# Sliding-window attention in rounds of three items instead of one or two, ahead of two expert layers

## The chip, the cores and the metric

The kernel runs on one NeuronCore of a Trainium2 chip. The metric is the device time of one execution in microseconds (us), as the median of several runs. Engines: PE is TensorE (matmuls and transposes; PEld its weight loads), DVE is VectorE, ACT is ScalarE, POOL is GpSimd, SP issues most DMAs. Each engine works through its own instructions in order; semaphores tie the engines together.

## The reference

Attention over q, k, v of shape (4 batches, 8 heads, 576 positions, 64 wide) in fp32, with a causal window of 128 positions and a linear distance bias per head; then a soft mixture of 8 experts with a balancing loop; then one dense layer pair.

```
scores = q @ k.T / sqrt(64)                       # per batch and head
mask   = (0 <= i - j) & (i - j < 128)
attn   = softmax(where(mask, scores - slope[h] * (i - j), -1e9))
x      = (attn @ v) laid out as (2304 tokens, 512)
P      = exp(x @ w_gate - max); 8 times: rows and columns of P scaled to fixed sums
x      = sum_e P[:, e] * (relu(x @ w1[e]) @ w2[e])      # w1[e] 512x1024, w2[e] 1024x512
h      = x @ w_in;  g = h, 0 or (h + 1)^2 / 4 by h's range
out    = g @ w_out
```

## The kernel before, in words

Matmuls that need precision are made of three (`mm3`, lines 74 to 76): high part by high part, high by low, low by high. The time falls into three stretches. Attention takes the first 223 us or so; the rest of a first expert unit and the balancing loop follow until about 272 us; the experts and the dense pair take what is left. The change touches attention alone.

**Items.** Attention is cut into 80 items: 16 head pairs `g` (4 per batch) times 5 blocks `i` of query rows (four of 128 rows, the last, `i == FULL`, of 64 rows, both heads of the pair stacked in one 128-row tile). Block 0 sees 128 keys, blocks 1 to 3 see 256, the last 192. An item goes through five steps:

- S, `a_scores`: matmuls into two PSUM banks, one per head (tags `s0`, `s1`); then DVE reads them with the bias added and the row minimum taken (L327).
- E, `a_exp`: ACT takes the exponential of each head (L336).
- N, `a_norm`: DVE makes the reciprocal of the row sums (L341, L342), POOL multiplies (L343).
- T, `a_turn`: PE transposes the item's weights into one bank of tag `t` (L355), which has two buffers; ACT copies out the first key block (L359), DVE the second (L361). An item of block 0 has only the first.
- O, `a_out`: PE multiplies by v (L375) into one bank of tag `o`; ACT copies the high part out (L383), DVE makes the low part (L386).

**Other work in a round.** P, `a_prep`: a pair's q and k are transposed (three parts: two with four transposes, one, the tail, with two) into a bank of tag `p` (one buffer), in the first batch also tag `g`; ACT makes the high part (L298), DVE the low (L301). Loads of later pairs (`a_load`) are issued on SP behind a pair's third part. B: one step of the weight preparation `u0_weights`. F: the filler, a few steps of a first expert unit (`unit0`: three matmuls a step, into the two banks of tag `g`); it may begin on a block of rows when enough items are through O (`step[0]`, first block after the 8th item), and gets 1.8 steps per item.

All eight PSUM banks are taken: `g` 2, `p` 1, `s0`, `s1`, `t` 2, `o` 1.

**Rounds.** The order of all engines' queues is written out by hand: in each round the letters of `START` or `ORDER` are emitted in sequence, and `BEHIND` says how many items an operation stands behind S. A round takes one item while the item's number is under 20, then two:

```
START, ORDER, NSTART = "EBSNFPOT", "ESONTPBFP", 20
BEHIND = [{"S": 0, "E": 1, "N": 1, "T": 3, "O": 4}, {"S": 0, "E": 2, "N": 2, "T": 4, "O": 6}]
two = new >= NSTART
new += 1 + two
```

That makes 20 rounds of one, 30 of two, and 3 more to empty the pipeline.

Of the kernel before, what the change touches and what calls it, by code (L numbers as in the profile page):

```python
# [19 lines left out]
P = 128  # L20
# [9 lines left out]
def attn_moe_ffn(ctx: ExitStack, tc, q, k, v, w_gate, w1, w2, w_in, w_out, out):  # L30
# [171 lines left out]
    TAIL = [slice(0, P // 2), slice(P // 2, P)]  # L202
    nat, QK, st, atT = {}, {}, {}, {}
    tails, QT = {}, {}

    def tail_at(g):
        return g if g < NPAIR else NPAIR + g % 2
# [9 lines left out]
    def a_load(g, ap):  # L217

        b, hp = divmod(g, NPAIR)
        for nm, src in (("q", q), ("k", k)):  # L220
            t = ap.tile([P, FULL, P], F32, tag=f"n{nm}", bufs=2, name=f"n{nm}")
            for j in range(2):
                sj = src[b, 2 * hp + j]
                nc.sync.dma_start(out=t[:, 0:FULL, j * D:(j + 1) * D],
                                  in_=sj[0:FULL * P, :].rearrange("(c p) d -> p c d", p=P))
            nat[g, nm] = t
        tail_load(g)

    def rows(src, b, i, h0, h1):
        x, n = QB[i]  # L230
# [26 lines left out]
        for g in range(NPAIR):  # L257
            tail_load(g)

    def a_prep(g, ap, part):  # L260

        b, hp = divmod(g, NPAIR)
        if part == 0:
            r = B - 1 - hp // 2
            for n, nm in enumerate("qk"):
                if r > b:
                    x, c0 = (xh, xl)[hp % 2], r * SQ
                    QK[g, nm] = [x[:, 2 * n + m, c0:c0 + SQ] for m in range(2)]
                else:
                    QK[g, nm] = [ap.tile([P, SQ], F32R, tag=f"{nm}{x}", bufs=3, name=f"{nm}{x}") for x in "hl"]  # L270

        if b == 0 and count[0] % 3:
            ps = ps_pools[0].tile([P, 512], F32, tag="g", bufs=2, name="pst")
        else:
            ps = ps_pools[0].tile([P, 512], F32, tag="p", bufs=1, name="pst")
        count[0] += 1
        if part == 2:
            todo = [("q", FULL, NQ, 0), ("k", FULL, NQ, P)]
            for n, nm in enumerate("qk"):
                nc.tensor.transpose(ps[:, n * P:(n + 1) * P], tails[nm, tail_at(g)], ident)  # L280
            QT[g] = [ap.tile([P, P], F32R, tag=f"qt{x}", bufs=4, name=f"qt{x}") for x in "hl"]
        elif b == 0:
            todo = [("q", 2 * part, 2 * part + 2, 0), ("k", 2 * part, 2 * part + 2, 256)]
        else:
            todo = ([("q", 0, 4, 0)], [("k", 0, 4, 0)])[part]
        for nm, i0, i1, c0 in todo if part < 2 else ():
            for i in range(i0, i1):
                x, n = QB[i]
                nc.tensor.transpose(ps[:, c0 + x - i0 * P:c0 + x - i0 * P + n], nat[g, nm][:n, i, :], ident[:n, :n])
        low = []  # L290
        for nm, i0, i1, c0 in todo:
            scale = SCALE if nm == "q" else 1.0
            s0, s1 = QB[i0][0], QB[i1 - 1][0] + QB[i1 - 1][1]
            h, l = (t[:, s0:s1] for t in QK[g, nm])
            pc = ps[:, c0:c0 + s1 - s0]
            if part == 2 and nm == "q":
                (h, l), pc = QT[g], ps[:, 0:P]
            nc.scalar.activation(h, pc, AF.Copy, scale=scale)  # L298
            low.append((l, pc, scale, h.bitcast(F32), ALU.mult, ALU.subtract))
        for x in low:  # L300
            nc.vector.scalar_tensor_tensor(*x)  # L301

    def a_scores(some, ap, bias):

        PS = [ps_pools[0].tile([P, 2, 2 * P], F32, tag=f"s{j}", bufs=1, name="pss") for j in range(2)]
        made = []
        for x, (g, i) in enumerate(some):
            q0, nq = QB[i]
            k0 = max(0, q0 - P)
            nk = q0 + nq - k0  # L310
            made.append((nq, nk, P if i == 0 else 0))
            (qh, ql), (kh, kl) = QK[g, "q"], QK[g, "k"]
            if i == FULL:
                mm3(PS[0][:, x, :nk], *QT.pop(g), kh[:, k0:k0 + nk], kl[:, k0:k0 + nk], True, True)
                continue
            for j in range(2):
                hs = slice(j * D, (j + 1) * D)
                mm3(PS[j][:nq, x, :nk], qh[hs, q0:q0 + nq], ql[hs, q0:q0 + nq], kh[hs, k0:k0 + nk], kl[hs, k0:k0 + nk],
                    True, True)
        for x, (g, i) in enumerate(some):  # L320
            nq, nk, c0 = made[x]
            h0 = 2 * (g % NPAIR)
            s = ap.tile([P, 2, 2 * P], F32, tag="s", bufs=6, name="s")
            mx = ap.tile([P, 8], F32, tag="mx", bufs=8, name="mx")
            nj = 1 if i == FULL else 2
            for j in range(nj):
                nc.vector.tensor_tensor_reduce(  # L327
                    out=s[:, j, :nk], in0=PS[j][:, x, :nk],
                    in1=bias[:, h0 + j, c0:c0 + nk] if nj == 2 else tbias[:, g % NPAIR, :], scale=-1.0,
                    scalar=3.0e38, op0=ALU.add, op1=ALU.min, accum_out=mx[:, j:j + 1])  # L330
            st[g, i] = (s, mx, nk, nj)
# [14 lines left out]
    def a_turn(g, i, ap):  # L346

        s, mx, nk, nj = st.pop((g, i))
        kbs = [i] if i == 0 else [i - 1, i]
        ps = ps_pools[0].tile([P, 2, 2, P], F32, tag="t", bufs=2, name="psat")  # L350
        at = ap.tile([P, 2, 2, P], F32, tag="at", bufs=4, name="at")
        for c, kb in enumerate(kbs):
            n = QB[kb][1]
            for j in range(nj):
                nc.tensor.transpose(ps[:n, c, j, :], s[:, j, c * P:c * P + n], ident)  # L355
        for c, kb in enumerate(kbs):
            n = QB[kb][1]
            if c == 0:
                nc.scalar.activation(at[:n, c, 0:nj, :], ps[:n, c, 0:nj, :], AF.Copy)  # L359
            else:  # L360
                nc.vector.tensor_copy(at[:n, c, 0:nj, :], ps[:n, c, 0:nj, :])  # L361
        atT[g, i] = (at, kbs)

    def a_out(some):
        PS = ps_pools[0].tile([P, 2, P], F32, tag="o", bufs=1, name="pso")
        low = []
        for x, (g, i) in enumerate(some):
            b, hp = divmod(g, NPAIR)
# [416 lines left out]

    START, ORDER, NSTART = "EBSNFPOT", "ESONTPBFP", 20
    BEHIND = [{"S": 0, "E": 1, "N": 1, "T": 3, "O": 4}, {"S": 0, "E": 2, "N": 2, "T": 4, "O": 6}]
    SHARE = 1.8  # L790
    PREP0 = [-1, 3, 4, 0, 5, 6, 1, 7, 8, 2, 9, 10]
    PREP = [11, 14, 17, 20, 29, 34, 37, 41, 53, 56, 59, 67]
    LAG = (5, 4, 4, 5, 6, 6, 6, 6)
    with tc.manual_schedule():
        nc.gpsimd.memset(small, 0.0)
# [2 lines left out]
        make_identity(nc, ident)  # L798

        NG = B * NPAIR  # L800
        items = []
        for b in range(B):
            for c in ((0, 1), (2, 3, 4)) if b < B - 1 else (range(NQ),):
                items += [(g, i) for g in range(b * NPAIR, (b + 1) * NPAIR) for i in c]
        NI = len(items)
        preps = sorted((y, *divmod(n, 3)) for n, y in enumerate(PREP0) if n)
        preps += [(PREP[g - NPAIR] + x, g, x) for g in range(NPAIR, NG) for x in range(3)]

        blocks = [(7, 0, 256), (19, 256, 256), (27, 512, 256), (39, 768, 384), (47, 1152, 256), (59, 1408, 256),
                  (79, 1664, 384), (79, 2048, 256)]  # L810
# [6 lines left out]
        with tc.tile_pool(name="ac", bufs=1, side="right") as ac, tc.tile_pool(name="ap", bufs=2, side="right") as ap, \  # L817
# [72 lines left out]
            while done["O"] < NI:  # L890
                s += 1
                step[0] = done["O"]
                two = new >= NSTART
                new += 1 + two
                order = ORDER if two else START
                for pos, op_ in enumerate(order):
                    some = ()
                    if op_ in done:
                        end = max(done[op_], min(new - BEHIND[two][op_], NI))
                        some = items[done[op_]:end]  # L900
                        done[op_] = end
                    if op_ == "S":
# [8 lines left out]
                        if s == 3:  # L911
                            for x in range(NPAIR, NPAIR + 2):
                                a_load(x, ap)
                        if s == 2:
                            fast.append(u0_weights(wp))
                        if s == 9:
# [8 lines left out]
                        for x in some:  # L925
                            a_turn(*x, ap)
                    elif op_ == "B":
                        advance(fast, 2 * (1 + two))
                    elif op_ == "F":
                        credit += SHARE * (1 + two) / order.count("F")  # L930
                        while credit >= 1.0:
                            credit -= 1.0
                            state = next(work)
                            if state == "wait":
                                credit = 0.0
                    elif op_ == "P":
                        if s == max(PREP0) + 1:
                            p0.close()
                            hp = p1b.enter_context(tc.tile_pool(name="hp", bufs=1))
                            op = p1b.enter_context(tc.tile_pool(name="op", bufs=2))  # L940
                        for _, pg, x in [y for y in preps if y[0] < new][:1]:
                            preps.pop(0)
                            a_prep(pg, ap, x)
                            if x == 2 and NPAIR <= pg < NG - 2:
                                a_load(pg + 2, ap)
                    elif op_ == "O" and some:
                        a_out(some)
                        for g, i in some:
# [109 lines left out]
```

## Time and profile before

| | us |
|---|---|
| median of 3 runs | 2064.2 (2062.78 to 2064.44) |
| profiled execution | 2063.22 |
| its span, first to last instruction | 2061.5 |
| PE busy in the span | 2039.0 (99%) |
| DVE, ACT, POOL busy | 1250.0, 703.7, 485.0 |

The profile comes from one execution. A busy PE counts a matmul from its start to its modelled end, and these overlap; how close PE is to its best is seen from the distance between the starts of neighbouring matmuls, not from its busy share.

### The profile page before, as it was taken

What the parts mean: (1) busy time and instruction counts of PE and PEld (TensorE: products, weight loads), DVE (VectorE), ACT (ScalarE), POOL (GpSimd) and SP (SyncE); (2) the same over time, 40 slices, a digit from 0 to 9 for tenths busy, and PEclk for the clock granted to TensorE, in tenths of its full rate; (3) what the DMA queues carried; (4) which work ended last, traced back from release to release, by engine and by line L of the source; (5) the groups of instructions that cost most, each with busy time, mean ns of one, the idle gap of its engine ahead of it and who ended that gap; (6) DMA issues with size and microseconds to landing.
All of it is one profiled execution on the core that took longest, in us unless ns stands there. A gap on an engine that the chain in (4) does not pass through costs nothing.

```text
span 2061.5 us, 30122 instructions
## 1 busy us (share of the span) xinstructions
PE 2039.0 (99%) x11071; PEld 1830.9 (89%) x11071; DVE 1250.0 (61%) x2916; ACT 703.7 (34%) x1657; POOL 485.0 (24%) x522
## 2 busy tenths in 40 slices
PE   7999999999999999999999999999999999999999
PEld 5888889989989889889999899899899898998998
DVE  6766656545545766666566665666665565656645
ACT  6767443333333332112112132122121134553543
POOL 5333347666666601111111100101110000000000
PEclk9999999999999999999999999999999999999999
DMA  7331448767776657667667566676675454555552
GB/s 158 85 86 48 141 160 296 264 247 252 257 257 246 255 209 280 232 233 251 232 229 247 216 220 247 230 257 224 225 263 190 181 192 184 198 208 184 219 189 108
DMA packets 180132, 432.83 MB, mean 210 GB/s; under 512 B 69648, under 2 KB 93712, under 8 KB 179984
## 3 DMA queue, kind: packets, MB, share of 16 engines
q1 hardware_dynamic: 168080, 411.37, 57.0%
q10 hardware_dynamic: 11904, 19.53, 2.9%
q8 instruction: 87, 1.43, 0.3%
q14 instruction: 61, 0.50, 0.1%
HBM read 311.44 MB, written 119.01 MB: 209 GB/s over the span
## 4 chain that ended last, share of the span: by engine, by line
PE 93%; DVE 3%; DMA 1%; SPq 1%; issue 1%; ACT 0%; POOL 0%; ACTq 0%; DVEq 0%; POOLq 0%
PE psg L74 16%; PE psg L76 16%; PE psg L75 16%; PE psc L74 4%; PE psd L74 4%; PE psc L75 4%; PE psc L76 4%; PE psd L75 4%; PE psd L76 4%; PE psb L74 3%; PE psa L75 3%; PE psb L75 3%; PE psb L76 3%; PE psa L76 3%; PE psa L74 3%; PE pso L375 2%
## 5 line engine op out<-in xcount | busy, mean ns | idle before, releaser
L74 PE MATMUL psg<-w2h,hh 128*128 128x512 f32 x1368 | 533.7, 390 | 0.1
L76 PE MATMUL psg<-w2h,hl 128*128 128x512 f32 x1368 | 532.8, 389 | 0.0
L75 PE MATMUL psg<-w2l,hh 128*128 128x512 f32 x1368 | 532.2, 389 | 0.0
L734 DVE SCALAR_TENSOR_TENSOR acc<-psg,pt,acc 128x512 f32<-128x512 f32 x252 | 187.9, 749 | 247.7 <-PE psg L76 245.9
L76 PEld LDWEIGHTS psg<-w2h,hl 128*128 128x128 f32 x1368 | 256.8, 188 | 53.4
L74 PEld LDWEIGHTS psg<-w2h,hh 128*128 128x128 f32 x1368 | 256.8, 188 | 51.8 <-DVE acc L734 1.3
L75 PEld LDWEIGHTS psg<-w2l,hh 128*128 128x128 f32 x1368 | 256.9, 188 | 50.8
L662 ACT ACTIVATE hh<-c 128x384 fp32r<-128x384 f32 x270 | 140.9, 522 | 90.9 <-DVE c L700 57.4
L664 DVE SCALAR_TENSOR_TENSOR hl<-c,hh 128x384 fp32r<-128x384 f32 x270 | 161.2, 630 | 0.0
L74 PE MATMUL psc<-xh,w1h 128*128 128x384 f32 x456 | 155.2, 340 | 1.6 <-DVE u L689 1.6
L76 PE MATMUL psc<-xh,w1l 128*128 128x384 f32 x456 | 154.9, 340 | 0.0
L74 PE MATMUL psd<-sh,w1h 128*128 128x384 f32 x456 | 153.6, 337 | 1.2 <-DVE c L692 0.8
L75 PE MATMUL psc<-xl,w1h 128*128 128x384 f32 x456 | 154.8, 339 | 0.0
L75 PE MATMUL psd<-sl,w1h 128*128 128x384 f32 x456 | 153.0, 336 | 0.0
L76 PE MATMUL psd<-sh,w1l 128*128 128x384 f32 x456 | 152.9, 335 | 0.0
L683 ACT ACTIVATE p<-psa 128x384 f32<-128x384 f32 x57 | 28.1, 494 | 355.7 <-PE psa L76 353.2
L80 POOL TENSOR_TENSOR dl<-e,dh 128x128 fp32r<-128x128 f32 (+1 forms) x64 | 43.2, 683 | 353.2 <-ACT dh L79 345.0
L80 POOL TENSOR_TENSOR w2l<-raw,w2h 128x512 fp32r<-128x512 f32 x60 | 81.4, 1379 | 119.6 <-ACT w2h L79 119.6
L686 DVE TENSOR_TENSOR u<-psb,p 128x384 f32<-128x384 f32 x57 | 31.7, 557 | 111.9 <-PE psb L76 91.5
L79 ACT ACTIVATE dh<-e 128x128 fp32r<-128x128 f32 (+1 forms) x64 | 23.7, 387 | 220.3 <-DVE e L162 216.2
L343 POOL TENSOR_TENSOR s<-s,mx 128x512 f32<-128x512 f32 (+2 forms) x80 | 66.7, 850 | 124.9 <-DVE mx L341 77.1
L74 PEld LDWEIGHTS psd<-sh,w1h 128*128 128x128 f32 x456 | 85.7, 188 | 2.4 <-DVE c L692 1.4
(220 smaller groups left out, 4071.9 us busy)
## 6 DMA issues: line engine op xcount, KB each, us to landing
w1h<-wd1h SPq DMA_DIRECT2D x84, 896.0 KB, 4.7
w1l<-wd1l SPq DMA_DIRECT2D x84, 896.0 KB, 6.8
w2h<-wd2h SPq DMA_DIRECT2D x84, 512.0 KB, 5.1
w2l<-wd2l SPq DMA_DIRECT2D x84, 512.0 KB, 5.9
raw<-in_moe_w SPq DMA_DIRECT2D x60, 512.0 KB, 4.4
wd1h<-w1h SPq DMA_DIRECT2D x30, 896.0 KB, 6.0
wd1l<-w1l SPq DMA_DIRECT2D x30, 896.0 KB, 6.5
wd2h<-w2h SPq DMA_DIRECT2D x30, 512.0 KB, 6.0
```

What stands on the lines that cost most here:

```text
L74: nc.tensor.matmul(ps, lhsT=lh, rhs=rh, start=first, stop=False, skip_group_check=on)
L75: nc.tensor.matmul(ps, lhsT=lh, rhs=rl, start=False, stop=False, skip_group_check=on)
L76: nc.tensor.matmul(ps, lhsT=ll, rhs=rh, start=False, stop=last, skip_group_check=on)
L79: nc.scalar.activation(h, x, AF.Copy)
L80: eng.tensor_tensor(l, x, h.bitcast(F32), ALU.subtract)
L343: nc.gpsimd.tensor_tensor(s[:, 0:nj, :nk], s[:, 0:nj, :nk], mx[:, 6:6 + nj].unsqueeze(2).to_broadcast([P, nj, nk]), ALU.mult)
L375: nc.tensor.matmul(PS[hs, x, :nq], lhsT=nat[b, "v", kb][:n, (2 * hp + j) * D:(2 * hp + j + 1) * D], rhs=at[:n, c, 0, TAIL[j]] if i == FULL ...
L662: nc.scalar.activation(h, c, AF.Relu)
L664: V.scalar_tensor_tensor(l, c, 0.0, h.bitcast(F32), ALU.max, ALU.subtract)
L683: nc.scalar.activation(p1, pa, AF.Copy)
L686: V.tensor_tensor(u2, pb, p1, ALU.add)
L734: nc.vector.scalar_tensor_tensor(a, ps, sc, a, ALU.mult, ALU.add)
```

## The change

From the ninth round on a round takes up to three items. The items of a batch are regrouped: blocks 0 and 1 of its pairs are mixed so that a round's score tiles fill a 512-column bank per head, and blocks 2, 3 and FULL of one pair make a round; the FULL scores go to the bank of tag `p`. The last batch mixes differently. Behind the same first 8 rounds of one there are 25 rounds (22 with three items, 3 with two), then 3 to empty the pipeline. `BEHIND` counts rounds now.

In a round the first E takes at most two items and the second, `e`, the third, with an N behind each. All P of a round stand in one place, behind T and these; a second and third P of a round use the banks of tag `t`. There is one P list per round number (`PREP`), and the loads of the pair after next are issued behind part 1 (the tails behind part 2). The third item of a round, where it is a narrow one, gets smaller tiles (`short`). The shares of the filler and its gates stay.

```diff
-        if b == 0 and count[0] % 3:
-            ps = ps_pools[0].tile([P, 512], F32, tag="g", bufs=2, name="pst")
-        else:
-            ps = ps_pools[0].tile([P, 512], F32, tag="p", bufs=1, name="pst")
+        if part < 2 and g < NPAIR and count[0] % 3:
+            tag = "g"
+        ps = ps_pools[0].tile([P, 512], F32, tag=tag, bufs=1 if tag == "p" else 2, name="pst")
...
-        PS = [ps_pools[0].tile([P, 2, 2 * P], F32, tag=f"s{j}", bufs=1, name="pss") for j in range(2)]
+        PS = [ps_pools[0].tile([P, 512], F32, tag=f"s{j}", bufs=1, name="pss") for j in range(2)]
...
             if i == FULL:
-                mm3(PS[0][:, x, :nk], *QT.pop(g), kh[:, k0:k0 + nk], kl[:, k0:k0 + nk], True, True)
+                pp = ps_pools[0].tile([P, 512], F32, tag="p", bufs=1, name="psf")
+                mm3(pp[:, :nk], *QT.pop(g), kh, kl, True, True)
...
-        ps = ps_pools[0].tile([P, 2, 2, P], F32, tag="t", bufs=2, name="psat")
-        at = ap.tile([P, 2, 2, P], F32, tag="at", bufs=4, name="at")
+        ps = ps_pools[0].tile([P, 512], F32, tag="t", bufs=2, name="psat").rearrange("p (c j q) -> p c j q", c=2, j=2)
+        if (g, i) not in short:
+            at = ap.tile([P, 2, 2, P], F32, tag="at", bufs=3, name="at")
+        else:
+            at = ap.tile([P, 2 * P], F32, tag="at1", bufs=2, name="at")
...
-        PS = ps_pools[0].tile([P, 2, P], F32, tag="o", bufs=1, name="pso")
+        PS = ps_pools[0].tile([P, 4, P], F32, tag="o", bufs=1, name="pso")
...
-    START, ORDER, NSTART = "EBSNFPOT", "ESONTPBFP", 20
-    BEHIND = [{"S": 0, "E": 1, "N": 1, "T": 3, "O": 4}, {"S": 0, "E": 2, "N": 2, "T": 4, "O": 6}]
+    START, ORDER = "EBSNFPOT", "ESONTeNPBF"
+    BEHIND = [{"S": 0, "E": 1, "N": 1, "T": 3, "O": 4}, {"S": 0, "E": 1, "N": 1, "T": 2, "O": 3}]
...
+        steps = []
         for b in range(B):
+            x = [[(b * NPAIR + n, i) for i in range(NQ)] for n in range(NPAIR)]
+            if b == 0:
+                steps += [[x[n][i]] for n in range(NPAIR) for i in range(2)]
+            elif b < B - 1:
+                steps += [[x[0][0], x[1][0], x[0][1]], [x[2][0], x[3][0], x[1][1]], [x[2][1], x[3][1]]]
+            if b < B - 1:
+                steps += [x[n][2:] for n in range(NPAIR)]
+            else:
+                steps += [[x[0][0], x[0][1], x[1][0]], x[0][2:], [x[1][1], x[1][2], x[1][4]],
+                          [x[1][3], x[2][0], x[3][0]], [x[2][1], x[2][2], x[2][4]], [x[2][3], x[3][1], x[3][4]], x[3][2:4]]
...
+                    if op_ == "E" and two:
+                        part = 2
+                    op_ = op_.upper()
...
+                        if part:
+                            end = min(end, done[op_] + part)
...
-                        for _, pg, x in [y for y in preps if y[0] < new][:1]:
-                            preps.pop(0)
-                            a_prep(pg, ap, x)
-                            if x == 2 and NPAIR <= pg < NG - 2:
-                                a_load(pg + 2, ap)
+                        for n, (pg, x) in enumerate(PREP.get(s, ())):
+                            a_prep(pg, ap, x, "t" if n else "p")
+                            if NPAIR <= pg < NG - 2:
+                                if x == 1:
+                                    a_load(pg + 2, ap)
+                                elif x == 2:
+                                    tail_load(pg + 2)
```

## Rows read from the trace of the kernel before

**Rows 1.** The page: busy share of PE; the chain that ended last, by engine.
```profile
PE 2039.0 (99%) x11071; PEld 1830.9 (89%) x11071; DVE 1250.0 (61%) x2916; ACT 703.7 (34%) x1657; POOL 485.0 (24%) x522
PE 93%; DVE 3%; DMA 1%; SPq 1%; issue 1%; ACT 0%; POOL 0%; ACTq 0%; DVEq 0%; POOLq 0%
```

**Rows 2.** Windows: stretch, its length, busy time per engine (instructions), clock, DMA.
```profile
31.50:34.50 3.00, 0.35 (x2) 0.12 (x2) 1.07 (x4) 2.27 (x8) 1.57 (x2) 0.88 0.62 178
34.50:39.50 5.00, 4.97 (x27) 3.46 (x28) 3.39 (x18) 3.96 (x15) 3.77 (x5) 0.50 0.92 193
39.50:44.70 5.20, 5.20 (x44) 3.80 (x43) 4.54 (x20) 4.81 (x18) 3.81 (x5) 0.89 0.17 66
66.00:222.70 156.70, 156.28 (x1446) 132.86 (x1446) 105.85 (x528) 109.61 (x408) 51.01 (x62) 1.00 0.28 66
```

**Rows 3.** Waits of PE over the span: total us, times, longest.
```profile
PE pso L375 <- DVE xl L386: 2.7, 1, 2.7
...
PE pss L74 <- DVE mx L327: 1.8, 1, 1.8
```

**Rows 4.** PE's timeline, one round of two: start, us to end, instruction.
```profile
129.41 0.34 PE L74 MATMUL pss<-kh,qh 64*128 64x128 f32 x2
...
130.30 0.88 PE L375 MATMUL pso<-at,nv 128*64 128x128 f32 x12
131.10 0.87 PE L355 MATMUL psat<-ident,s 128*128 128x128 f32 x6
131.73 0.36 PE L74 MATMUL psg<-xh,w0h 128*128 128x256 f32 x1
131.93 0.28 PE L75 MATMUL psg<-xl,w0h 128*128 128x256 f32 x1
132.05 0.28 PE L76 MATMUL psg<-xh,w0l 128*128 128x256 f32 x1
...
132.97 0.39 PE L74 MATMUL pss<-xh 64*128 64x256 f32 x2
```

**Rows 5.** PE's timeline, one round of one.
```profile
60.58 0.39 PE L74 MATMUL pss<-xl 64*128 64x256 f32 x2
...
61.14 0.39 PE L74 MATMUL psg<-xh,w0h 128*128 128x256 f32 x1
...
62.48 0.66 PE L375 MATMUL pso<-at,nv 128*64 128x128 f32 x8
63.07 0.66 PE L355 MATMUL psat<-ident,s 128*128 128x128 f32 x4
63.48 0.33 PE L74 MATMUL pss<-xl,qth 128*128 128x192 f32 x1
```

**Rows 6.** DVE's timeline in the round of rows 4.
```profile
130.50 0.29 DVE L327 CUSTOM_DVE_ANT_0 s<-pss,bias 128x128 f32<-128x128 f32 x1 [0.82 <-PE pss L76]
...
130.93 0.42 DVE L327 CUSTOM_DVE_ANT_0 s<-pss,bias 128x256 f32<-128x256 f32 x1
131.27 0.09 DVE L327 DVE_READ_ACCUMULATOR2_ANT mx<- 128x1 f32 x1
...
131.70 0.49 DVE L386 TENSOR_TENSOR xl<-pso,xh 128x128 fp32r<-128x128 f32 x2
132.10 0.16 DVE L341 TENSOR_SCALAR mx<-mx 128x2 f32<-128x2 f32 x1
...
132.64 0.40 DVE L361 COPY at<-psat 128x256 f32<-128x256 f32 x1
```

**Rows 7.** ACT's timeline in the same round.
```profile
131.22 0.45 ACT L383 ACTIVATE xh<-pso 128x128 fp32r<-128x128 f32 x2 [0.25 <-PE pso L375]
131.64 0.82 ACT L359 ACTIVATE at<-psat 128x256 f32<-128x256 f32 x2
```

**Rows 8.** The tile psat from 60 to 223 us: copies of the second key block, ns min/median/max.
```profile
L361 DVE COPY at<-psat x54: 261/404/425, 61.2 to 220.3; 128x256 f32<-128x256 f32 x40, 64x128 f32<-64x128 f32 x14
```

**Rows 9.** DMA issues from 60 to 223 us: KB each, median us to landing.
```profile
nq<-in_q SPq DMA_DIRECT2D x15, 128.0 KB, 3.0
```

More of the change, by code (lines that the diff above doesn't have):

```diff
@@ L204, in attn_moe_ffn @@
     tails, QT = {}, {}
+    short = []
     def tail_at(g):
@@ L226, in a_load @@
             nat[g, nm] = t
-        tail_load(g)
     def rows(src, b, i, h0, h1):
@@ L258, in first_load, with a_prep @@
             tail_load(g)
-    def a_prep(g, ap, part):
+    def a_prep(g, ap, part, tag="p"):
         b, hp = divmod(g, NPAIR)
@@ L280, in a_prep @@
                 nc.tensor.transpose(ps[:, n * P:(n + 1) * P], tails[nm, tail_at(g)], ident)
-            QT[g] = [ap.tile([P, P], F32R, tag=f"qt{x}", bufs=4, name=f"qt{x}") for x in "hl"]
+            QT[g] = [ap.tile([P, P], F32R, tag=f"qt{x}", bufs=3, name=f"qt{x}") for x in "hl"]
         elif b == 0:
@@ L303, in a_scores @@
     def a_scores(some, ap, bias):
-        PS = [ps_pools[0].tile([P, 2, 2 * P], F32, tag=f"s{j}", bufs=1, name="pss") for j in range(2)]
-        made = []
-        for x, (g, i) in enumerate(some):
+        PS = [ps_pools[0].tile([P, 512], F32, tag=f"s{j}", bufs=1, name="pss") for j in range(2)]
+        made, c1 = [], 0
+        for g, i in some:
             q0, nq = QB[i]
@@ L310, in a_scores @@
             nk = q0 + nq - k0
-            made.append((nq, nk, P if i == 0 else 0))
             (qh, ql), (kh, kl) = QK[g, "q"], QK[g, "k"]
+            kh, kl = kh[:, k0:k0 + nk], kl[:, k0:k0 + nk]
             if i == FULL:
-                mm3(PS[0][:, x, :nk], *QT.pop(g), kh[:, k0:k0 + nk], kl[:, k0:k0 + nk], True, True)
+                pp = ps_pools[0].tile([P, 512], F32, tag="p", bufs=1, name="psf")
+                mm3(pp[:, :nk], *QT.pop(g), kh, kl, True, True)
+                made.append((nk, 0, [pp[:, :nk]]))
                 continue
+            banks = [x[:nq, c1:c1 + nk] for x in PS]
+            made.append((nk, P if i == 0 else 0, banks))
+            c1 += nk
             for j in range(2):
                 hs = slice(j * D, (j + 1) * D)
[L318 to L321, printed above, removed]
+                mm3(banks[j], qh[hs, q0:q0 + nq], ql[hs, q0:q0 + nq], kh[hs], kl[hs], True, True)
+        for (g, i), (nk, c0, banks) in zip(some, made):
             h0 = 2 * (g % NPAIR)
-            s = ap.tile([P, 2, 2 * P], F32, tag="s", bufs=6, name="s")
-            mx = ap.tile([P, 8], F32, tag="mx", bufs=8, name="mx")
-            nj = 1 if i == FULL else 2
+            nj = len(banks)
+            if (g, i) not in short:
+                s = ap.tile([P, 2, 2 * P], F32, tag="s", bufs=6, name="s")
+            else:
+                s = ap.tile([P, 2 * P], F32, tag="s1", bufs=3, name="s").rearrange("p (j k) -> p j k", j=nj)
+            mx = ap.tile([P, 8], F32, tag="mx", bufs=12, name="mx")
             for j in range(nj):
                 nc.vector.tensor_tensor_reduce(
-                    out=s[:, j, :nk], in0=PS[j][:, x, :nk],
+                    out=s[:, j, :nk], in0=banks[j],
                     in1=bias[:, h0 + j, c0:c0 + nk] if nj == 2 else tbias[:, g % NPAIR, :], scale=-1.0,
@@ L349, in a_turn @@
         kbs = [i] if i == 0 else [i - 1, i]
-        ps = ps_pools[0].tile([P, 2, 2, P], F32, tag="t", bufs=2, name="psat")
-        at = ap.tile([P, 2, 2, P], F32, tag="at", bufs=4, name="at")
+        ps = ps_pools[0].tile([P, 512], F32, tag="t", bufs=2, name="psat").rearrange("p (c j q) -> p c j q", c=2, j=2)
+        if (g, i) not in short:
+            at = ap.tile([P, 2, 2, P], F32, tag="at", bufs=3, name="at")
+        else:
+            at = ap.tile([P, 2 * P], F32, tag="at1", bufs=2, name="at")
+            at = at.rearrange("p (c j q) -> p c j q", c=len(kbs), j=nj)
         for c, kb in enumerate(kbs):
@@ L782, in x2_t @@
         nc.vector.tensor_tensor(xl[:, :, cs], ps, xh[:, :, cs].bitcast(F32), ALU.subtract)
-    START, ORDER, NSTART = "EBSNFPOT", "ESONTPBFP", 20
-    BEHIND = [{"S": 0, "E": 1, "N": 1, "T": 3, "O": 4}, {"S": 0, "E": 2, "N": 2, "T": 4, "O": 6}]
+    START, ORDER = "EBSNFPOT", "ESONTeNPBF"
+    BEHIND = [{"S": 0, "E": 1, "N": 1, "T": 3, "O": 4}, {"S": 0, "E": 1, "N": 1, "T": 2, "O": 3}]
     SHARE = 1.8
-    PREP0 = [-1, 3, 4, 0, 5, 6, 1, 7, 8, 2, 9, 10]
-    PREP = [11, 14, 17, 20, 29, 34, 37, 41, 53, 56, 59, 67]
+    PREP = {n: [x] for n, x in enumerate([(1, 0), (2, 0), (3, 0), (0, 1), (0, 2), (1, 1), (1, 2), (2, 1)])}
+    PREP.update({8: [(2, 2), (3, 1)], 9: [(3, 2), (4, 0), (4, 1)], 10: [(5, 0), (5, 1)], 11: [(6, 0), (6, 1)],
[4 rows of a table added]
     LAG = (5, 4, 4, 5, 6, 6, 6, 6)
@@ L800, in attn_moe_ffn @@
         NG = B * NPAIR
-        items = []
+        steps = []
         for b in range(B):
-            for c in ((0, 1), (2, 3, 4)) if b < B - 1 else (range(NQ),):
-                items += [(g, i) for g in range(b * NPAIR, (b + 1) * NPAIR) for i in c]
+            x = [[(b * NPAIR + n, i) for i in range(NQ)] for n in range(NPAIR)]
[5 more added lines that the diff above has]
+                steps += [x[n][2:] for n in range(NPAIR)]
+            else:
+                steps += [[x[0][0], x[0][1], x[1][0]], x[0][2:], [x[1][1], x[1][2], x[1][4]],
+                          [x[1][3], x[2][0], x[3][0]], [x[2][1], x[2][2], x[2][4]], [x[2][3], x[3][1], x[3][4]], x[3][2:4]]
+        NSTART = 2 * NPAIR
+        items = [x for y in steps for x in y]
         NI = len(items)
-        preps = sorted((y, *divmod(n, 3)) for n, y in enumerate(PREP0) if n)
-        preps += [(PREP[g - NPAIR] + x, g, x) for g in range(NPAIR, NG) for x in range(3)]
+        for y in steps[2 * NPAIR:]:
+            short.extend([x for x in y if x[1] in (0, FULL)][-1:])
+        until = [sum(len(y) for y in steps[:x + 1]) for x in range(len(steps))]
         blocks = [(7, 0, 256), (19, 256, 256), (27, 512, 256), (39, 768, 384), (47, 1152, 256), (59, 1408, 256),
@@ L892, in attn_moe_ffn @@
                 step[0] = done["O"]
-                two = new >= NSTART
-                new += 1 + two
+                two = s >= NSTART
+                size = len(steps[min(s, len(steps) - 1)])
+                new = until[min(s, len(steps) - 1)]
                 order = ORDER if two else START
                 for pos, op_ in enumerate(order):
-                    some = ()
+                    some, part = (), 0
+                    if op_ == "E" and two:
+                        part = 2
+                    op_ = op_.upper()
                     if op_ in done:
-                        end = max(done[op_], min(new - BEHIND[two][op_], NI))
+                        end = s - BEHIND[two][op_]
+                        end = max(done[op_], until[min(end, len(steps) - 1)] if end >= 0 else 0)
+                        if op_ == "O":
+                            end = min(end, done["T"])
+                        if op_ == "N":
+                            end = min(end, done["E"])
+                        if part:
+                            end = min(end, done[op_] + part)
                         some = items[done[op_]:end]
@@ L913, in attn_moe_ffn @@
                                 a_load(x, ap)
+                                tail_load(x)
                         if s == 2:
@@ L927, in attn_moe_ffn @@
                     elif op_ == "B":
-                        advance(fast, 2 * (1 + two))
+                        advance(fast, 2 * size)
                     elif op_ == "F":
-                        credit += SHARE * (1 + two) / order.count("F")
+                        credit += SHARE * size
                         while credit >= 1.0:
@@ L936, in attn_moe_ffn @@
                     elif op_ == "P":
-                        if s == max(PREP0) + 1:
+                        if s == NSTART + 2:
                             p0.close()
```

4 rows, old and new, of the table PREP are left out of this document.

## The prediction

> **What bounds the kernel now.** I read the page first: PE is busy 99% of the span and holds 93% of the chain that ended last [rows 1]. A busy PE proves little, so the windows came next: from 66 to 222.7 us, where attention runs in rounds of two beside the filler, PE is busy 156.28 of 156.70 us at full clock, ACT 109.61, DVE 105.85, POOL 51.01 [rows 2]. Then the waits of PE over the whole span: the longest that touch attention are 2.7 and 1.8 us, once each, and none is of the transposes on their bank (no row of psat <- DVE or ACT) [rows 3]. So PE's own queue sets the time here, in its written order; what PE idles or wastes in attention is added to the end, since the work behind it is PE's too. The timelines show what a round wastes [rows 4, 5], and what the other engines do between an output and the next copy [rows 6, 7].
>
> **Fewer rounds: the gain.** PE loses time where it goes from one kind of work to the next. Rows 4 and 5 give it by subtraction. Scores: one item 0.56 us (60.58 to 61.14), two items 0.89 (129.41 to 130.30), so an item is 0.33 and 0.23 is fixed. Outputs: eight matmuls 0.59, twelve 0.80, so four are 0.21 and 0.17 is fixed. Turns: four 0.41, six 0.63, 0.11 each, fixed -0.03. Filler: nine matmuls take 1.24 (131.73 to 132.97) at 0.12 apart, fixed 0.16. Together 0.53 us a round. Behind the common first eight there were 12 + 30 + 3 = 45 rounds, now 25 + 3 = 28: 17 x 0.53 = **-9.0 us**, bounds -7 and -11 (a preparation that stood behind the filler and now stands behind the turns changes kind less often, too).
>
> **The third turn: the loss.** A turn needs a bank of tag t, and there are two. With two items a round, each turn finds a bank emptied a round ago. With three, the third must wait until the first turn's bank has been copied out in the same round: the left half by ACT, the right half by DVE. Both engines work in order, and ahead of DVE's copy stand the score reads, the low parts of the outputs, and the sums of the two items of the first N. Counting from the end of the outputs on PE (131.10 in rows 4): ACT starts the high parts 0.12 later (131.22) [rows 7]; DVE starts the low parts at 131.70, 0.60 later, just behind its last score read [rows 6], and could have started at about 0.46 (0.12, one high part of 0.24, and a signal of 0.1 as from PE to ACT); I take 0.53. Two low parts take 0.40 (131.70 to 132.10), three 0.60. The sums of two items take 0.54 (132.10 to 132.64). The copy takes 0.40, which is also the median of 54 [rows 6, 8]. With 0.12 for the signal to PE the bank is free 0.53 + 0.60 + 0.54 + 0.40 + 0.12 = 2.19 us behind the outputs. PE has two turns of four transposes to do before it needs it: 8 x 0.11 = 0.88. The rest, **1.3 us**, PE stands. The lower bound is 1.0 (the copy of 0.26 in rows 8 and an earlier start), the upper 1.5: six score reads at 0.35 (130.93 to 131.27) instead of four let DVE come later.
>
> Which rounds? Three items with a first turn that has a right half: the four rounds of blocks 2, 3, FULL in each of the first three batches, and five of the seven of the last batch: 17. 17 x 1.3 = +22.1 us (17.0 to 25.5). In five more rounds the first turn is of block 0 and has only ACT's half: 0.12, three high parts at 0.21 (131.22 to 131.64 for two) 0.63, one copy 0.41 (0.82 for two), signal 0.12: 1.28, against turns of 4 x 0.11 = 0.44 (6 x 0.11 = 0.66 in one round): 4 x 0.84 + 0.62 = **+4.0 us** (2 to 5). The part of E that was put behind T keeps ACT out of the way for this; had it stood ahead, ACT's copies would be later still. Queued behind the waiting transposes are the preparations and the whole filler of that round, which need nothing from the copies. None can step ahead.
>
> On this the Trainium skill speaks against the change: Perfetto Trace Analysis, section Optimization Strategy, says that a gap that repeats on the engine that should be saturated can mean too little PSUM for the next tile. The trace of before shows no such gap at the turns [rows 3], and going by its rows alone the sum would end with the gain, 2055; by the page's reading the gap comes once a round, and the sum is the one below. The skill's PSUM — Partial Sum Buffer, section Engine vs sequencer instructions, adds that matmuls start in program order; if the filler could pass the waiting turn, it would cost nothing.
>
> **Edits priced at nothing.** FULL scores in the bank of tag p: the same three matmuls; the preparation of the round before has been emptied behind one filler of 5 matmul triples, which covers it; without cover it is a wait like the 1.8 us of scores on DVE [rows 3], in the three rounds without filler only. Preparations in bank t: the second turn's copy is the next on DVE behind the first's, 0.3 us later, while PE does the third turn and the first preparation; without that cover up to 0.5 us in some 15 rounds. Loads behind part 1: some follow only one round ahead of their use; 3.0 us to landing [rows 9] and about 1 us of issue stand against a round of three of some 7 us or more (1.5 times the 3.56 of rows 4, plus the stand, and more with wide filler); if a round is shorter, 1 us each. The smaller tiles keep as many items alive as are in flight, no wait. POOL has 51 of 157 us of work [rows 2]. Filler steps not done in attention are done right behind it.
>
> **The start.** At 31.5 to 34.5 us PE is nearly empty, and then runs 5 us at clock 0.50 [rows 2], the lower of its two levels, 1.2 GHz. This stall (2.7 us on the output bank, [rows 3]) comes before anything that the change moves. From the ninth round to the first filler there are three rounds instead of four, but of three items each. ACT was busy 4.81 of 5.20 us there [rows 2]: it is the limit, and it must now do exponentials of more items before the first filler comes. PE has those items' scores and turns to do meanwhile, so most is only moved. I take +1 us, between -1 and +6.
>
> **Sum.** The profiled execution took 2063.2 (span 2061.5): 2063.2 - 9.0 + 22.1 + 4.0 + 1 = 2081.3. The median of the runs lies 1.0 above that execution: **2082 us**, 0.9% slower. By the bounds this case reaches from 2064.2 - 11 + 17 + 2 - 1 = 2071 to 2064.2 - 7 + 25.5 + 5 + 6 = 2094.
>
> **Rivals.**
> 1. Faster: the third turn does not wait, because the first turn's right half is out by the time the second turn ends. For it: DVE is idle a third of the stretch [rows 2]. Against: the order of its queue, in which the copy stands behind low parts that cannot begin before the outputs end. It decides at 9.0 / 22 rounds = 0.4 us a round: DVE's 2.19 would have to be 1.3. Without any wait the time is 2064.2 - 9.0 = 2055. Chance 0.22.
> 2. No change: a wait of half a microsecond (the sums of N already done, an early start of the low parts), 2064.2 - 9.0 + 22 x 0.5 = 2066. Chance 0.08.
> 3. Slower still: rounds 9 to 11 run dry. ACT's 2.4 us per round of one (4.81 us for about two) makes up to 6 us in a round of three against some 4.5 of PE (scores 1.2, outputs 1.4, turns 1.1, preparations 0.8); 3 x 1.5 = 4.5 us, and if the clock falls again for 5 us, as behind the gap at 31.5, half of that once more: 2082 + 4.5 + 2.5 - 1 = 2088, or 2095 with the upper bound of the turns. Chance 0.12.
> 4. My forecast, 2071 to 2094, about 2082. Chance 0.58.
>
> Within 0.2% (4 us) counts as no change, about what a measurement of this kernel can tell. Slower 0.58 + 0.12 = 0.70, same 0.08, faster 0.22. For 8 in 10 the range has to take in part of the faster case: 2056 to 2094.
>
> **What would show it.** In the profile after: a new wait of PE, psat <- DVE at L361's copy (about 17 times, 1.3 us) and psat <- ACT at L359's (5 times, 0.8 us); 25 stretches of scores behind the first eight; fixed losses of 0.5 us a round as before; ACT nearly full and PE with gaps from 35 to 50 us. The prediction is wrong if DVE's copy of the first turn begins before the second turn's transposes end, or if PE's waits at the turns sum to less than 9 us.

## The result and the profile after

The changed kernel takes 2084.73 us (median of 5 runs, 2083.47 to 2090.4) against 2064.2: ratio 1.0104 over all runs (1.0099 by the medians), 95% interval 1.0093 to 1.0116. It is slower by about 21 us; the forecast was 2082. The profiled execution took 2083.72, with a span of 2082.0; its lines below are set against [rows 1 to 7] of before, whose span was 2061.5.

The waits of PE come first: total us, times, longest. Before, no row of them named a turn [rows 3].

```profile
PE psat L364 <- DVE at L370: 22.2, 16, 2.6
...
PE psat L364 <- ACT at L368: 2.7, 6, 0.6
...
PE pst L288 <- DVE mx L346: 0.9, 1, 0.9
```

Twenty-two new waits, one in each round with three items: 16 end with DVE's copy of the right half, 6 with ACT's of the left. Now the windows (columns as in [rows 2]); the second stretch is attention from the first filler to the last outputs.

```profile
39.50:56.60 17.10, 11.74 (x120) 9.51 (x117) 14.32 (x65) 12.87 (x49) 9.89 (x11) 1.00 0.46 109
56.60:238.40 181.80, 159.82 (x1508) 138.58 (x1506) 113.85 (x554) 113.55 (x435) 55.98 (x67) 0.99 0.25 59
228.00:231.00 3.00, 1.59 (x20) 1.22 (x16) 0.97 (x7) 2.53 (x12) 0.00 (x0) 1.00 0.00 0
231.00:234.00 3.00, 2.35 (x14) 2.39 (x14) 1.10 (x4) 0.28 (x1) 2.04 (x2) 0.71 0.00 0
```

PE, which idled 0.4 of 156.7 us before [rows 2], idles 22 of 181.8. One round shows where. PE's timeline of a round of three:

```profile
113.34 0.33 PE L74 MATMUL pss<-xh 64*128 64x128 f32 x2
...
114.57 1.47 PE L384 MATMUL pso<-at,nv 128*64 128x128 f32 x24
115.97 1.09 PE L364 MATMUL psat<-ident,s 128*128 128x128 f32 x8
118.31 0.41 PE L364 MATMUL psat<-ident,s 128*128 128x128 f32 x2 [1.24 <-DVE at L370]
118.56 0.60 PE L288 MATMUL pst<-ident,nk 128*128 128x128 f32 x4
...
119.13 0.37 PE L74 MATMUL psg<-xh,w0h 128*128 128x256 f32 x1
...
122.43 0.33 PE L74 MATMUL pss<-kh,qh 64*128 64x128 f32 x2
```

The first two turns are eight transposes, 0.11 apart behind the first. The eighth has a row of its own in a narrower window:

```profile
116.79 0.27 PE L364 MATMUL psat<-ident,s 128*128 128x128 f32 x1
```

A ninth could have started at 116.90; the third turn starts at 118.31. So by starts PE loses 1.41 us. The view says 1.24, because it counts from the modelled end of the eighth; it is short by 0.16 us in every such wait. By starts the sixteen waits come to 24.8 us and the six to 3.7. The preparations and the filler stand behind them. DVE and ACT in the same round:

```profile
115.97 0.42 DVE L332 CUSTOM_DVE_ANT_0 s<-pss,bias 128x256 f32<-128x256 f32 x1
116.32 0.08 DVE L332 DVE_READ_ACCUMULATOR2_ANT mx<- 128x1 f32 x1
116.68 0.62 DVE L395 TENSOR_TENSOR xl<-pso,xh 128x128 fp32r<-128x128 f32 x3 [0.28 <-ACT xh L392]
117.22 0.16 DVE L346 TENSOR_SCALAR mx<-mx 128x2 f32<-128x2 f32 x1
...
117.76 0.73 DVE L370 COPY at<-psat 128x256 f32<-128x256 f32 x2
```

```profile
116.09 0.56 ACT L392 ACTIVATE xh<-pso 128x128 fp32r<-128x128 f32 x3 [1.30 <-PE pso L384]
116.73 0.76 ACT L368 ACTIVATE at<-psat 128x256 f32<-128x256 f32 x2
```

From the end of the outputs (115.97): high parts +0.12, low parts +0.71, sums +1.25, copy +1.79, third turn +2.34. The chain is the one of the prediction, with 2.34 us in place of 2.19, and PE's two turns take 0.93 us of it in place of 0.88.

### The profile page after: what moved, and what is told of

It reads as the page before. It is cut to its first block, busy times and chain, and to the rows that moved or that the text cites. A ratio compares the mean times of both kernels' runs of the same rounds, so it can differ in the third digit from the quotient of the medians.

```text
span 2082.0 us, 30063 instructions
## 1 busy us (share of the span) xinstructions
PE 2036.1 (98%) x11071; PEld 1833.7 (88%) x11071; DVE 1247.3 (60%) x2916; ACT 700.7 (34%) x1657; POOL 486.1 (23%) x522
## 4 chain that ended last, share of the span: by engine, by line
PE 93%; DVE 3%; ACT 2%; issue 1%; SPq 1%; DMA 0%; POOL 0%; POOLq 0%; DVEq 0%; ACTq 0%
PE psg L76 16%; PE psg L74 16%; PE psg L75 16%; PE psc L74 4%; PE psc L76 4%; PE psc L75 4%; PE psd L75 4%; PE psd L74 4%; PE psd L76 4%; PE psb L74 3%; PE psa L75 3%; PE psb L75 3%; PE psa L76 3%; PE psb L76 3%; PE psa L74 3%; PE pso L384 1%
## 5 line engine op out<-in xcount | busy, mean ns | idle before, releaser
L74 PEld LDWEIGHTS psc<-xh,w1h 128*128 128x128 f32 x456 | 85.7, 188 | 2.0 <-DVE u L698 1.9
```

What stands on the lines that cost most here:

```text
L74: nc.tensor.matmul(ps, lhsT=lh, rhs=rh, start=first, stop=False, skip_group_check=on)
```

## The experiments

Theory A is the prediction's: the third turn waits for the first turn's bank, behind DVE's queue, and this outweighs the saving of fewer rounds. Rival B: the regrouping itself costs (late filler, dry rounds), and the wait would only move. "Before" runs on the same chip in each group: 2063.93 for runs 1 to 4, 2063.34 for runs 6 to 9, 2064.24 for runs 5 and 10; beside the changed kernel it took 2064.2. So differences to the changed kernel are sure to about 1 us. In brackets stand the ratio to before and its 95% interval.

**1. The wait filled with work (e1_fill).** The third turn goes behind half of the filler.

```diff
-    START, ORDER = "EBSNFPOT", "ESONTeNPBF"
+    START, ORDER = "EBSNFPOT", "ESONTeNFtPBF"
...
-                    if op_ == "E" and two:
+                    if op_ in "ET" and two:
...
-                        credit += SHARE * size
+                        credit += SHARE * size / order.count("F")
```

> The changed kernel with its third turn moved behind half of the round's filler (order E S O N T e N F t P B F, two turns ahead of the first half of the filler, the third behind it). Theory A (the third turn waits for the first turn's bank, and this wait is the loss): the wait is filled with work, so about 25 of its 28 us go, and one more change of kind a round comes, 25 x 0.16 = 4 us: 2062 to 2067. Rival B (the regrouping itself costs: late first filler, dry rounds 9 to 11, DVE too late for whatever comes next on PE, so that the wait only moves): 2078 or more, with a new wait of PE of about 1 us a round at another place.

2062.63 (0.9996, 0.9987 to 1.0005). 22 us went with nothing but the order changed, and no wait of about 1 us a round came up elsewhere. Six waits at the turns are left; 4.9 of their 5.8 us come from one round without filler (2.6) and the last two rounds (0.9 and 1.3):

```profile
PE psat L364 <- DVE at L370: 5.8, 6, 2.6
```

**2. DVE's queue shortened (e2_sums_late).** Both N behind the turns.

```diff
-    START, ORDER = "EBSNFPOT", "ESONTeNPBF"
+    START, ORDER = "EBSNFPOT", "ESOTeNPBF"
```

> The changed kernel with both N behind the turns (E S O T e N P B F): the sums of two items, 0.54 us, no longer stand ahead of DVE's copy of the first turn. Theory A with the prediction's queue of DVE: 16 or 17 waits shorter by 0.54, so 8.6 to 9.2 us less: about 2076, and PE's wait psat <- DVE falls from 22.2 to about 13 us. Rival B, or a wait that hangs on something else than DVE's queue: 2083 to 2086.

2073.63 (1.0048, 1.0033 to 1.0063), 11 us less than the changed kernel. The waits on DVE, 13.6 for the expected 13:

```profile
PE psat L364 <- DVE at L370: 13.6, 16, 1.7
...
PE psat L364 <- ACT at L368: 2.7, 6, 0.6
```

8.6 us of 22.2 went, 0.54 each, and the six waits on ACT stayed as they were: the wait hangs on what stands ahead of the copy in DVE's queue. Of the other 2 us, some 1.5 are a fall of PE's clock behind the last wait, which the profile of the changed kernel has and the profile of this run has not (last section).

**3. The wait put into the kernel before (e3_one_bank).** Rounds of one and two, one turn bank.

```diff
-        ps = ps_pools[0].tile([P, 2, 2, P], F32, tag="t", bufs=2, name="psat")
+        ps = ps_pools[0].tile([P, 2, 2, P], F32, tag="t", bufs=1, name="psat")
```

> The kernel before, rounds of one and two, with one turn bank instead of two: the second turn of a round must wait for the first one's copies. Theory A: in 20 of its 30 rounds of two the first turn has a right half, wait 0.53 + 0.40 + 0.54 + 0.40 + 0.12 - 0.44 = 1.55 us; in 10 it has ACT's half alone, 0.12 + 0.42 + 0.41 + 0.12 - 0.22 = 0.85: 31 + 8.5 = 40 us more, about 2104. Rival B (such a wait is mostly taken back later): 2070 or less.

2108.88 (1.022, 1.0203 to 1.0237), 45 us more. The rounds of two had been free of waits; with the turn bank short they are not.

```profile
PE psat L355 <- DVE at L361: 22.2, 15, 1.8
PE psat L355 <- POOL s L343: 8.6, 6, 1.6
PE psat L355 <- ACT at L359: 6.9, 10, 1.1
```

Fifteen rows are put down to DVE and six to POOL where 20 to DVE were forecast. The starts settle it. One of the rows that name POOL, with DVE's copy of the same round:

```profile
104.05 0.52 PE L355 MATMUL psat<-ident,s 128*128 128x128 f32 x3 [1.42 <-POOL s L343]
103.50 0.40 DVE L361 COPY at<-psat 128x256 f32<-128x256 f32 x1
```

The turn starts 0.15 us behind the end of DVE's copy (103.90), and so do all 21, whichever name the row has. POOL multiplies an item two items ahead of its turn, so its work in this round is for the next one. So 21 waits hang on DVE, 30.8 us for the 31 forecast, and ten on ACT, 6.9 for 8.5.

**4. A third turn bank (e4_three_banks).** The bank of tag p joins tag t; preparations behind the filler.

```diff
-        ps = ps_pools[0].tile([P, 512], F32, tag=tag, bufs=1 if tag == "p" else 2, name="pst")
+        ps = ps_pools[0].tile([P, 512], F32, tag=tag, bufs=2 if tag == "g" else 3, name="pst")
...
-                pp = ps_pools[0].tile([P, 512], F32, tag="p", bufs=1, name="psf")
+                pp = ps_pools[0].tile([P, 512], F32, tag="t", bufs=3, name="psf")
...
-        ps = ps_pools[0].tile([P, 512], F32, tag="t", bufs=2, name="psat").rearrange("p (c j q) -> p c j q", c=2, j=2)
+        ps = ps_pools[0].tile([P, 512], F32, tag="t", bufs=3, name="psat").rearrange("p (c j q) -> p c j q", c=2, j=2)
...
-    START, ORDER = "EBSNFPOT", "ESONTeNPBF"
+    START, ORDER = "EBSNFPOT", "ESONTeNBFP"
...
-                            a_prep(pg, ap, x, "t" if n else "p")
+                            a_prep(pg, ap, x, "t")
```

> The changed kernel with the bank of tag p given to the turns: three banks of tag t for full scores, turns and preparations, and the preparations behind the filler (E S O N T e N B F P). Theory A: no turn waits in its own round; about 28 us less, up to 3 us back where a preparation is now needed by the very next scores: 2057 to 2062, faster than the kernel before by the saving of fewer rounds. Rival B: 2078 or more.

2061.0 (0.9984, 0.9975 to 0.9994). No row psat <- DVE at is left, and no row psat <- ACT at. With the turns' waits gone the larger rounds do pay, 3 us net here.

**5. The order of run 4 without its bank (e9_order_only).**

```diff
-    START, ORDER = "EBSNFPOT", "ESONTeNPBF"
+    START, ORDER = "EBSNFPOT", "ESONTeNBFP"
```

> The changed kernel with the preparations behind the filler and nothing else changed (E S O N T e N B F P, banks as they are: two for turns, one of tag p). It takes the run with three banks apart. Theory A: the third turn waits as before, 16 x about 1.4 us, so 2082 to 2087. Rival (the place of the preparations, not the bank, made the difference): 2061 to 2070.

2089.31 (1.0122, 1.0105 to 1.0139): the third bank made run 4, not the place of the preparations. It is 2 us over the expected bound, and the waits name a cause that had been priced at nothing: the full scores of the next round find the bank of tag p not yet emptied of the preparation ahead of them. The other scores wait for preparations too (pss, 1.7 us in all). How much of the 2 us each is worth was not separated.

```profile
PE psat L364 <- DVE at L370: 21.3, 16, 2.1
...
PE psat L364 <- ACT at L368: 2.7, 6, 0.6
...
PE psf L74 <- DVE xl L300: 1.4, 2, 0.8
PE psf L74 <- DVE kl L300: 1.3, 1, 1.3
```

In the changed kernel the filler covers this, all but 0.2 us.

**6. The exponentials in one part (e5_one_part).**

```diff
-    START, ORDER = "EBSNFPOT", "ESONTeNPBF"
+    START, ORDER = "EBSNFPOT", "ESONTPBF"
...
-                        part = 2
+                        part = 3
```

> The changed kernel with the exponentials in one part again (order E S O N T P B F, E and N of all three items). Theory A: the sums of the third item, 0.27 us, stand ahead of DVE's copy too, 16 x 0.27 = 4.3 us, and ACT has one item's exponentials (1.0 us) more ahead of the high parts of the outputs, which is late only where they take longer than scores and outputs on PE: 2088 to 2092. Rival (the split of the exponentials is worth nothing, or is itself a part of the loss): 2086 or less.

2090.81 (1.0135, 1.012 to 1.015). The split was worth 6 us, 4.1 of them in the same wait and 1.9 in preparations that need a bank of tag t (0.8 us in the changed kernel):

```profile
PE psat L364 <- DVE at L370: 26.3, 16, 2.9
...
PE pst L288 <- DVE at L370: 2.7, 2, 1.5
```

**7. Rounds of three from the twelfth on (e6_late_start).** Three more items in rounds of one.

```diff
-                steps += [x[n][2:] for n in range(NPAIR)]
+                steps += [x[n][2:] for n in range(NPAIR)] if b else [[y] for y in x[0][2:]] + [x[n][2:] for n in range(1, NPAIR)]
...
-        NSTART = 2 * NPAIR
+        NSTART = 2 * NPAIR + 3
```

> The changed kernel with rounds of three from the twelfth round on instead of the ninth (the first pair's blocks 2, 3, FULL in rounds of one; preparations two rounds later). Theory A: two rounds more (+1.1), one third turn fewer (the longest, -2.8), fewer preparations that stand in rounds without filler (-1 to -2): 2080 to 2083. Rival B (the dry start is the main loss): 2075 or less.

2084.02 (1.0098, 1.0081 to 1.0115): no gain clear of noise, 1 us above the range of A and far from B. The profile offers a reason that neither had. Its window from 34 to 57 us:

```profile
34.00:57.00 23.00, 21.12 (x141) 16.74 (x141) 16.15 (x72) 15.22 (x52) 11.57 (x12) 0.65 0.45 109
```

PE was busy 21.1 of 23 us there at a mean clock of 0.65, so at the lower level most of the time; the kernel before had it low from 34.5 to 39.5 and in part of the next 5 us [rows 2]. In the changed kernel it reads 1.00 from 39.5 to 56.6. One execution shows it, the longest of the four (2086.14); the two shortest, 2082.66 and 2082.81, lie within the range of A. Whether the clock makes that difference stays open.

**8. Rounds of one throughout (e8_single), on the kernel before.**

```diff
-    START, ORDER, NSTART = "EBSNFPOT", "ESONTPBFP", 20
+    START, ORDER, NSTART = "EBSNFPOT", "ESONTPBFP", 1000
```

> The kernel before with rounds of one throughout: 80 + 4 rounds instead of 53. The same work, only more changes of kind on PE. With 0.53 us a round: 31 x 0.53 = 16 us more, 2080 (2074 to 2085). Rival (the fixed part is an artefact of the subtraction, or is hidden by the filler): 2064 to 2068. A wait of PE of over 1 us a round would spoil the reading.

2084.01 (1.01, 1.0084 to 1.0115): 20.7 us for 31 rounds, 0.67 a round (0.56 to 0.77 by the interval), without waits at the turns:

```profile
45.00:241.00 196.00, 196.00 (x1630) 148.90 (x1629) 131.28 (x597) 128.61 (x463) 59.90 (x70) 1.00 0.25 61
```

PE is "busy" 196.00 of 196.00 us here and yet 20 us slower for the same work: the loss lies between the starts of matmuls, and only there it can be read.

**9. Three banks, later start, tight preparations a round earlier (e7_both).** The edits of runs 4 and 7, and a plan in which no preparation is needed by the very next scores.

```diff
+    PREP.update({10: [(3, 2), (4, 0), (4, 1)], 11: [(5, 0), (5, 1)], 12: [(6, 0), (6, 1)], 13: [(7, 0), (7, 1)],
...
+                 19: [(9, 1), (10, 0)], 20: [(10, 1), (11, 0), (11, 1)], 21: [(8, 2)], 22: [(9, 2)], 23: [(10, 2)],
+                 24: [(11, 2)], 25: [(12, 0)], 26: [(12, 1), (13, 0), (13, 1)], 27: [(12, 2)], 28: [(13, 2), (14, 0)],
...
-                        if s == NSTART + 2:
+                        if s == NSTART:
```

> Three turn banks and preparations behind the filler, rounds of three from the twelfth on, and the preparations that the very next scores need put a round earlier. In the run with three banks about 9 us of gaps of PE over 0.36 us were left between 34 and 190 us; theory A: half of them go, 2055 to 2059, so 5 to 9 us faster than the kernel before. Rival (what is left is not of these places): 2060 to 2062.

2056.8 (0.9971, 0.9962 to 0.998): faster than both kernels, 6.5 us under before. Which of the later start and the new plan gave the 4 us against run 4 was not separated. Its turns in a round of three, on PE:

```profile
97.10 1.09 PE L384 MATMUL pso<-at,nv 128*64 128x128 f32 x16
98.12 1.36 PE L364 MATMUL psat<-ident,s 128*128 128x128 f32 x10
99.24 0.37 PE L74 MATMUL psg<-xh,w0h 128*128 128x256 f32 x1
```

Ten transposes take 1.12 us (98.12 to 99.24); in the changed kernel ten take 2.59 (115.97 to 118.56).

**10. Run 9 with the exponentials in one part (e10_whole).**

```diff
-    START, ORDER = "EBSNFPOT", "ESONTeNBFP"
+    START, ORDER = "EBSNFPOT", "ESONTBFP"
...
-                        part = 2
+                        part = 3
```

> The run with three banks and the later start, its exponentials and sums in one part (E S O N T B F P). Theory A: the split pays only because the third turn hangs on the copies; with three banks nothing on PE waits for them in the round, so no change: 2055 to 2059. Rival (the split pays by itself, ACT's exponentials holding up the high parts): 2061 or more, as the 6 us that it was worth in the changed kernel.

2057.72 (0.9969, 0.9957 to 0.998), no difference. The split was worth 6 us only while PE hung on the copies.

## Why the prediction was right

**The third turn.** Shown, by its removal in two ways (runs 1 and 4), by one term of its queue (run 2), and by putting it where it had not been (run 3). Its size was a little low: 16 waits of 1.55 on average by starts, 24.8 us, against 17 of 1.3, 22.1 us. In the round shown it is 1.41, and the term that was off is the start of the low parts, 0.71 us behind the outputs and not 0.53: I let DVE start after the first high part. In the row it starts 0.03 us behind the last of the three (116.09 + 0.56 = 116.65, then 116.68), and [rows 6, 7] had shown the same (131.22 + 0.45 = 131.67, then 131.70), though DVE's last score read ended there too. The six score reads, the reason for the upper bound, did not matter in this round: they end at 116.40. The other terms held: sums 0.54, copy and signal 0.55 for 0.52, low parts 0.54 for 0.60, two turns on PE 0.93 for 0.88.

Three waits are longer, and the prediction had no term for them. In the first (2.6 us by the view) 1.24 us of DVE's preparation of the gate weights stands ahead of its score reads. In the last two (1.6 and 2.05) ACT is still at its exponentials when the outputs end: in the last one the high parts start 0.95 us behind the outputs, not 0.12.

**Where only ACT's half counts.** Six waits of 0.45 by the view, 0.62 by starts, 3.7 us in all for 4.0, but one more of them and one fewer on DVE. In one round of the last batch the third turn is of block 0, which has a left half alone, so the prediction's count of 17 was one too high. That this turn needs only the left half emptied can be seen:

```profile
218.02 0.41 PE L364 MATMUL psat<-ident,s 128*128 128x128 f32 x2 [0.62 <-ACT at L368]
218.31 0.41 DVE L370 COPY at<-psat 128x256 f32<-128x256 f32 x1
```

The third turn starts 0.29 us before DVE begins to copy the right half of the first.

**Fewer rounds.** Right in kind and, if anything, too small: 0.53 by subtraction, 0.67 by run 8. That run makes rounds of one out of rounds of two; taken over to rounds of three, as an estimate, 17 rounds are worth some 9.5 to 13 us. The net gain with no third turn waiting was 3 us in run 4 and 6.5 in run 9.

**The sum.** -11.4 (17 x 0.67), +24.8, +3.7 and +1.5 for the fall of the clock (last section) make 18.6 of the 20.5 us between the two spans. For the rest the profile shows a part: from 39.5 to 56.6 us PE idles 5.4 us, 3.9 of them in two of the turn waits already counted. The +1 forecast for the start is of the size of what remains there. More cannot be said, because the start differs between the two executions in another way: before, the clock is low from 34.5 to 39.5 [rows 2]; in the changed kernel four transposes take 1.05 us at 28.80, where before they took 0.58 at 28.09, though the clock from 26 to 30 us reads 1.00. That the forecast came within 3 us is in part luck: 2.7 us too little for the turns and 2.4 too little for the saving nearly cancel.

Rival 3 (dry rounds) was not needed: run 7, which shortens them, gained nothing clear. Its upper figure of 2095 does not come out of its terms: with 25.5 and 5 us for the turns in place of 22.1 and 4.0 they give 2092. Rival 1 stands refuted by the first group of waits above: DVE's idle third is idle at other times than those at which PE needs it. One reading of [rows 3] was incomplete: PE also waited once for 3.7 us (a preparation, on POOL) and once for 1.9 (outputs, on the load of v), both in the first 22 us, ahead of what the change moves.

**Edits priced at nothing.** The preparations in bank t and the loads one round ahead made no wait over 0.9 us; the full scores in bank p cost 0.2 us in the changed kernel, but only under the cover that was named, as run 5 showed when it took the filler away from behind them.

## What to carry to other kernels

When a round is made larger, count for each rotating buffer how often it is taken within one round: with more uses than buffers, the last use waits for a copy of this round, and behind that copy's engine's whole queue. Price the wait from the end of the work that feeds that queue, term by term, and set it against what the larger round saves. If no buffer is to be had, put work that needs nothing between the uses; here that alone gave back 22 us.

## What the runs showed of the hardware that was not expected

The clock of PE fell near the end of attention. In the changed kernel the last turn wait is 2.05 us long, PE is busy 1.59 of 3 us from 228 to 231, and in the next 3 us the mean granted clock is 0.71 (rows above). PE's timeline there:

```profile
227.10 1.47 PE L384 MATMUL pso<-at,nv 128*64 128x128 f32 x24
228.50 1.09 PE L364 MATMUL psat<-ident,s 128*128 128x128 f32 x8
231.65 0.41 PE L364 MATMUL psat<-ident,s 128*128 128x128 f32 x2 [2.05 <-DVE at L370]
...
234.27 2.13 PE L384 MATMUL pso<-at,nv 128*64 128x128 f32 x24
236.34 1.09 PE L364 MATMUL psat<-ident,s 128*128 128x128 f32 x8
237.19 0.36 PE L74 MATMUL psg<-xh,w0h 128*128 128x256 f32 x1
```

Twenty-four output matmuls took 1.40 us (227.10 to 228.50) and, after that wait, 2.07 (234.27 to 236.34). Run 2 has the same work there behind a wait of 1.50 us:

```profile
221.53 0.41 PE L364 MATMUL psat<-ident,s 128*128 128x128 f32 x2 [1.50 <-DVE at L370]
...
223.25 1.47 PE L384 MATMUL pso<-at,nv 128*64 128x128 f32 x24
224.65 1.12 PE L364 MATMUL psat<-ident,s 128*128 128x128 f32 x8
225.52 0.37 PE L74 MATMUL psg<-xh,w0h 128*128 128x256 f32 x1
```

Its outputs took 1.40 us. From the third turn to the filler behind the next turns it needs 3.99 us (221.53 to 225.52), the changed kernel 5.54 (231.65 to 237.19). So that wait cost about 1.5 us more than its own length, by one execution of each. In the round of 118.31, with a wait of 1.24 us by the view, the filler behind it stands 0.12 apart, as in [rows 4].
